# FFN products as three one-pass products of 12-bit parts, in place of seven full-precision products for eight

## The chip, the cores and the metric

The kernel runs on one core of one Trainium2 chip. The core has five engines that work side by side: TensorE (PE, matrix products; its weight loads are listed as PEld), VectorE (DVE), ScalarE (ACT), GpSimd (POOL), and SyncE (SP), which here starts most of the transfers. Matrix products go to PSUM[...]. The metric is the time of one execution on the device, in microseconds (us); lower is better. Before the change it is 296.61 us, the median of three runs (296.38 to 301.45). The profiled execution, from which the rows below come, spanned 300.1 us.

## The reference, cut to what matters

Two parts run one after the other: a chunked state-space scan (batch 4, 8 heads, 768 tokens, head dimension 32, state 16), and on its output a feed-forward network (FFN) with a maximum over three products.

```python
# x (4, 8, 768, 32), a (4, 8, 768), B and C (4, 8, 768, 16); log_a = log(clip(a, 1e-6, 1))
for c in range(24):                                # chunks of 32 tokens in the reference
    cum = np.cumsum(la, axis=-1)
    L = np.exp(cum[..., :, None] - cum[..., None, :]) * causal
    y_intra = (Cc @ Bc.T * L) @ xc                 # within the chunk
    y_inter = (Cc @ state) * np.exp(cum)[..., None]    # from the chunks before
    y[:, :, sl] = y_intra + y_inter
    state = exp(sum(la)) * state + sum_j exp(cum[-1] - cum[j]) * outer(B[j], x[j])

xx = y.transpose(0, 2, 1, 3).reshape(3072, 256)
h = np.maximum(np.maximum(xx @ w1, xx @ w2), xx @ w3)   # w1, w2, w3: 256 x 768
out = h @ w_out                                         # w_out: 768 x 256
```

All of it is in 32-bit floating point. The weights arrive as 64-bit numbers, which the kernel itself decodes to 32 bits.

## The kernel before

It works in six blocks. Block c holds tokens 128c to 128c+127 of all four batches, so 512 tokens. The scan of block c+1 is woven into the FFN of block c, and the last product of the FFN (`out = h @ w_out`, here called the down product) of a block is done while the next block's FFN runs. The order of the instructions on each engine is the order of the program.

The first FFN products (the up products) of block 0 are plain: four 128 x 512 products for each weight and pair of column tiles. From the second block on they go by a scheme in which seven products of 256 columns take the place of eight, with sums of the weights and of the scan's output made beforehand, and sums of the results made afterwards:

```python
def weight_sums(k):                    # GpSimd, once for each of the 9 weight groups k
    nc.gpsimd.tensor_tensor(out=s1, in0=a21, in1=a22, op=ALU.add)
    nc.gpsimd.tensor_tensor(out=s3, in0=a11, in1=a21, op=ALU.subtract)
    nc.gpsimd.tensor_tensor(out=s2, in0=s1, in1=a11, op=ALU.subtract)
    nc.gpsimd.tensor_tensor(out=s4, in0=a12, in1=s2, op=ALU.subtract)

def products(c, k, which, first):
    for p, bank, half in which:
        nc.tensor.matmul(                                             # L628
            out=bank[:, half], lhsT=left(p, k), rhs=sides[c][p],
            start=(first and half == 0), stop=True, skip_group_check=True)

def early(c, k):
    A, B = (sum_bank(kind, [P, 2, HB]) for kind in "AB")              # HB = 256 tokens
    products(c, k, [(1, A, 0), (6, A, 1), (5, B, 0), (7, B, 1)], True)
    ...
    nc.scalar.copy(out=eu[:, 0], in_=A[:, 0])                         # L653
    nc.vector.tensor_tensor(out=eu[:, 1], in0=A[:, 1], in1=eu[:, 0], op=ALU.add)   # L654
    nc.vector.tensor_tensor(out=v, in0=B[:, 1], in1=eu[:, 1], op=ALU.add)          # L655
    nc.vector.tensor_tensor(out=t[:, 2], in0=B[:, 0], in1=v, op=ALU.add)           # L656

def late(c, k):
    products(c, k, [(2, A, 0), (3, B, 0), (4, B, 1)], False)
    if i == 0:
        nc.scalar.copy(out=m[:, 0], in_=A[:, 0])                                   # L667
    else:
        nc.vector.tensor_tensor(out=to[:, 0], in0=m[:, 0], in1=A[:, 0], op=ALU.max)  # L669
    nc.vector.tensor_tensor(                                                       # L670
        out=t[:, 0:2], in0=B, in1=eu[:, 1:2].to_broadcast([P, 2, HB]), op=ALU.add)
    if i > 0:
        return [lambda: nc.vector.tensor_tensor(                                   # L673
            out=to[:, 1:4], in0=m[:, 1:4], in1=t, op=ALU.max)]

def down_next(kind=ffn_bank):          # 3 products of 256 columns, 24 products per block
    ...
    for f in range(half * NQ, (half + 1) * NQ):
        nc.tensor.matmul(                                             # L691
            out=o[:, i], lhsT=hT[c][:, f, b * P:(b + 1) * P], rhs=wo_sb[:, f],
            start=(f == 0), stop=(f == NF - 1), skip_group_check=True)
    ...                                # then a copy to SBUF and a transfer to the output

for c in range(1, NC):                 # blocks 1 to 5
    for k in range(NW):                # 9 weight groups: 3 weights x 3 groups of 256 columns
        early(c, k)
        ...                            # a piece of the next block's scan, or down_next()
        maximum = late(c, k)
        if c == 1 and k + 2 < NW:
            weight_sums(k + 2)
        ...                            # more pieces, masks, loads
while downs:
    down_next(att_bank)                # the last block's down products, alone at the end
```

Of the scan, four kinds of work matter for the steps below. ACT takes the exponential of the decays, four instructions to a piece (L391). DVE multiplies the scores by the decays (L491). POOL masks the decays (L384). PE makes the scores (L483) and the scan's output y (L506, L519), which ACT copies out of PSUM (L543). In the decoding of the weights ACT (L175, L184), DVE (L176, L179, L188) and POOL (L185) take turns.

Of the kernel before, what the change touches and what calls it, by code (L numbers as in the profile page):

```python
# [10 lines left out]
BF16 = mybir.dt.bfloat16  # L11
U32 = mybir.dt.uint32
# [7 lines left out]
def kernel(  # L20
# [41 lines left out]

    SMALL, LARGE = 2.0 ** -15, 122880.0 - 2.0 ** -7

    const = ctx.enter_context(tc.tile_pool(name="const", bufs=1))
    raw = ctx.enter_context(tc.tile_pool(name="raw", bufs=2))
    att = ctx.enter_context(tc.tile_pool(name="att", bufs=2))
    ffn = ctx.enter_context(tc.tile_pool(name="ffn", bufs=2))
    wraw = ctx.enter_context(tc.tile_pool(name="wraw", bufs=10))
    wtmp = ctx.enter_context(tc.tile_pool(name="wtmp", bufs=3))  # L70
# [51 lines left out]
    def load(c, name):  # L122
        src, w = sources[name]
        t = blocks[c][name] = raw.tile([P, BH, w], FP32, tag="raw_" + name, name="raw_" + name)
        nc.sync.dma_start(  # L125
            out=t, in_=src[:, :, c * P:(c + 1) * P, :].rearrange("b h s n -> s (b h) n"))
# [3 lines left out]
    w_sb = [const.tile([P, KD, DF], FP32, name="w%d" % i) for i in range(3)]  # L130
    wo_sb = const.tile([P, NF, DM], FP32, name="wo")
# [4 lines left out]

    weight_jobs = []
    for f0 in range(0, DF, WCOL):
        for w, t in zip((moe_w1, moe_w2, moe_w3), w_sb):
            per = 1 if w.dtype == FP32 else 2  # L140
            src = words(w)[:, per * f0:per * (f0 + WCOL)]
            weight_jobs.append(
                (t[:, :, f0:f0 + WCOL], src.rearrange("(k p) f -> p k f", p=P), w.dtype))
    for o in range(0, NF, 2):
        weight_jobs.append(
            (wo_sb[:, o:o + 2],
             words(moe_w_out)[o * P:(o + 2) * P, :].rearrange("(o p) m -> p o m", p=P),
             moe_w_out.dtype))

    fetched = []  # L150

    def fetch():

        dst, src, dt = weight_jobs.pop(0)
        if dt == FP32:
            nc.sync.dma_start(out=dst, in_=src)
        else:
            rb = wraw.tile([P, 2, WCOL, 2], U32, tag="rb", name="rb")
            nc.sync.dma_start(out=rb.rearrange("p k f w -> p k (f w)"), in_=src)  # L159
            fetched.append((dst, rb))  # L160

    def decode_steps():


        dst, rb = fetched.pop(0)
        shape = [P, 2 * WCOL]
# [3 lines left out]
        def first():  # L170
# [3 lines left out]
            held["u"] = u = wtmp.tile(shape, U32, tag="w_u", name="w_u")  # L174
# [8 lines left out]
            r = wtmp.tile(shape, U32, tag="w_r", name="w_r")  # L183
# [19 lines left out]
    def sign():  # L203

        unsigned.pop(0)()

# [169 lines left out]
    def last_load(c):  # L376
        E = blocks[c]["E"] = raw.tile([HN, NB, P], FP32, tag="E", name="E")
# [21 lines left out]

    def scan_b(c, kind):  # L400
# [4 lines left out]
        st["BT"] = BT = att.tile([HN, NB, P], FP32, tag="BT", name="BT")  # L405
# [13 lines left out]
    def scan_c(c):  # L419
# [3 lines left out]
        st["CT"] = CT = att.tile([HN, NB, 2, P], FP32, tag="CT", name="CT")  # L423
        for g in range(2):
            nc.scalar.mul(CT[:, :, g], tr, parity[:, g:g + 1])
# [5 lines left out]
    def scan_cd(c):  # L431
# [3 lines left out]
        st["Cd"] = Cd = att.tile([HN, NB, P], FP32, tag="Cd", name="Cd")  # L435
        nc.vector.tensor_tensor(out=Cd, in0=st["trC"], in1=E, op=ALU.mult)

    def scan_bd(c):
        st = blocks[c]
        st["Bd"] = Bd = att.tile([P, BH, N], FP32, tag="Bd", name="Bd")  # L440
        nc.gpsimd.tensor_tensor(
            out=Bd, in0=st["B"], in1=from_j[c].unsqueeze(2).to_broadcast([P, BH, N]),
# [31 lines left out]
    def scan_scores(c, b0, banks=None):  # L474
# [4 lines left out]
        for i in range(2):  # L479
            b = b0 + i  # L480
            for r, s in banks.items():
# [3 lines left out]
                    rhs=st["CT"][rows, b].rearrange("p g i -> p (g i)"),  # L485
# [38 lines left out]
    def first_own(bs):  # L524
# [9 lines left out]
        if 0 not in yT:  # L534
            yT[0] = ffn.tile([P, KD, BLK], FP32, tag="yT", name="yT")
# [4 lines left out]
    def scan_y(c):  # L540
        yT[c] = ffn.tile([P, KD, BLK], FP32, tag="yT", name="yT")
        for t in range(KD):
            nc.scalar.copy(out=yT[c][:, t], in_=blocks[c]["y"][t].rearrange("p b i -> p (b i)"))  # L543

    def scan_sums(c):

        y11, y12, y21, y22 = (
            yT[c][:, k, r * HB:(r + 1) * HB] for k in range(2) for r in range(2))
        late = [blocks[c]["y"][k].rearrange("p b i -> p (b i)")[:, r * HB:(r + 1) * HB]
                for k in range(2) for r in range(2)]  # L550
        t = ysum[c % 2]
        later.extend(
            lambda k=k, a1=a1, a0=a0: nc.vector.tensor_tensor(  # L553
                out=t[:, k], in0=a1, in1=a0, op=ALU.subtract)
            for k, (a1, a0) in enumerate((
                (late[1], y11), (late[3], t[:, 0]), (late[3], y12), (late[2], t[:, 1]))))
        sides[c] = {1: y11, 2: y21, 3: y22, 4: t[:, 3], 5: t[:, 0], 6: t[:, 1], 7: t[:, 2]}


    hT = {}  # L560
    def h_of(c):
        if c not in hT:
            hT[c] = ffn.tile([P, NF, BLK], FP32, tag="h", name="h")
        return hT[c]

    def group(bank, i, f, halves):

        for r in halves:
            for k in range(KD):
                nc.tensor.matmul(  # L570
                    out=bank[:, r * HB:(r + 1) * HB],
                    lhsT=w_sb[i][:, k, f * P:(f + 1) * P],
# [3 lines left out]
    def whole_group(bank, i, f):  # L576
        for k in range(KD):
            nc.tensor.matmul(  # L578
                out=bank, lhsT=w_sb[i][:, k, f * P:(f + 1) * P], rhs=yT[0][:, k],
# [9 lines left out]
    NW = 3 * NQ  # L589
    ysum, wsum = [], {}  # L590

    def kilos(b):

        t = wraw.tile([P, 2, WCOL, 2], U32, tag="rb", name="rb").bitcast(FP32)
        return t.rearrange("p k f w -> p (k f w)").rearrange("p (a b) -> p a b", b=b)

    quarters = {}

    def places():
        for _ in range((NW + 1) // 2):  # L600
            t = kilos(P)
            for half in (t[:, 0:4], t[:, 4:8]):
                if len(wsum) < NW:
                    wsum[len(wsum)] = half
        ysum.extend(kilos(HB) for _ in range(2))

    def weight_sums(k):
        q, i = divmod(k, 3)
        a11, a12, a21, a22 = (
            w_sb[i][:, kk, (2 * q + g) * P:(2 * q + g + 1) * P]  # L610
            for g in range(2) for kk in range(2))
        s1, s2, s3, s4 = (wsum[k][:, j] for j in range(4))
        nc.gpsimd.tensor_tensor(out=s1, in0=a21, in1=a22, op=ALU.add)  # L613
        nc.gpsimd.tensor_tensor(out=s3, in0=a11, in1=a21, op=ALU.subtract)
        nc.gpsimd.tensor_tensor(out=s2, in0=s1, in1=a11, op=ALU.subtract)
        nc.gpsimd.tensor_tensor(out=s4, in0=a12, in1=s2, op=ALU.subtract)

    def left(p, k):
        if p in (1, 2, 4):
            q, i = divmod(k, 3)  # L620
            g, row = {1: (0, 0), 2: (0, 1), 4: (1, 1)}[p]
            f = 2 * q + g
            return w_sb[i][:, row, f * P:(f + 1) * P]
        return wsum[k][:, {5: 0, 6: 1, 7: 2, 3: 3}[p]]

    def products(c, k, which, first):
        for p, bank, half in which:
            nc.tensor.matmul(  # L628
                out=bank[:, half], lhsT=left(p, k), rhs=sides[c][p],
                start=(first and half == 0), stop=True, skip_group_check=True)  # L630

    later = []
# [6 lines left out]
    held = {}  # L639

    def early(c, k):
        q, i = divmod(k, 3)
        A, B = (sum_bank(kind, [P, 2, HB]) for kind in "AB")
        products(c, k, [(1, A, 0), (6, A, 1), (5, B, 0), (7, B, 1)], True)
        if i == 0:
            held["m"] = ffn.tile([P, 4, HB], FP32, tag="m", name="m")
# [331 lines left out]
```

## Time and profile before

| engine | busy us | share of the span | instructions |
|---|---|---|---|
| PE | 287.4 | 96% | 2024 |
| PEld | 225.1 | 75% | 2024 |
| DVE | 199.9 | 67% | 382 |
| ACT | 121.1 | 40% | 315 |
| POOL | 72.1 | 24% | 96 |

Busy time is that of the named engine in the span of 300.1 us. A 32-bit product stands in the trace as two pairs of weight load and product, so 315 products of the up side from block 1 on make 630 rows, and 144 down products make 288. Rows of the groups give the line of the kernel, the engine and operation, what is written and read, the shape, the number of instructions, then busy time and the mean length of one; after the bar stands the idle time just before them and what ended it. [...] DMA moved 28.13 MB in the span, at a mean of 94 GB/s.

### The profile page before, as it was taken

Reading aid. Unit: us, or ns where it says so; the run is one execution under the profiler, and the core shown is the slowest. Engines: PE = TensorE matmul, PEld = TensorE weight load, DVE = VectorE, ACT = ScalarE, POOL = GpSimd, SP = SyncE. Lnnn points to the kernel's source line nnn. Section 1 sums busy time; section 2 is a strip of 40 time slices with the busy share of each in tenths; the row PEclk is TensorE's granted clock in tenths of the full one; section 3 lists DMA queues with packets and bytes.
Section 4 is the critical chain, followed back from the end, with each engine's and each line's share of the span. In section 5 each row is a group of like instructions: output and inputs, shape, how many; then the busy total and the mean of one; then the engine's idle time right before and its main releaser. Section 6 shows DMA issues by size and latency. Waiting matters only on the chain.

```text
span 300.1 us, 5303 instructions
## 1 busy us (share of the span) xinstructions
PE 287.4 (96%) x2024; PEld 225.1 (75%) x2024; DVE 199.9 (67%) x382; ACT 121.1 (40%) x315; POOL 72.1 (24%) x96
## 2 busy tenths in 40 slices
PE   6679999999999999999999999999999999999995
PEld 4557435477677788888888888888887888888784
DVE  2752867989588556867676867676867676667540
ACT  2934687943672545334344334344330211011200
POOL 5241647468991600007000006000000000000000
PEclk9957999999999999999999999999999999999999
DMA  7989879969969105792007790001010001010101
GB/s 88 189 274 290 214 140 175 223 173 183 177 141 127 35 2 167 186 131 46 2 0 207 162 136 22 3 2 35 0 37 0 2 0 35 2 36 0 35 20 52
DMA packets 105049, 28.13 MB, mean 94 GB/s; under 512 B 75328, under 2 KB 101952, under 8 KB 105024
## 3 DMA queue, kind: packets, MB, share of 16 engines
q1 hardware_dynamic: 104144, 27.14, 45.6%
q10 hardware_dynamic: 880, 0.66, 0.7%
q8 instruction: 16, 0.26, 0.4%
q14 instruction: 9, 0.07, 0.1%
HBM read 24.54 MB, written 3.24 MB: 93 GB/s over the span
## 4 chain that ended last, share of the span: by engine, by line
PE 81%; DVE 7%; POOL 3%; DMA 3%; SPq 2%; issue 2%; ACT 1%; POOLq 0%; DVEq 0%; ACTq 0%
PE sumB L628 25%; PE o L691 19%; PE sumA L628 18%; PE up L578 5%; PE s L483 4%; DMA raw_x<-in_x_dram 3%; PE y L519 3%; DVE L L491 2%; PE up L570 2%; PE y L506 1%; POOL w_u L185 1%; PE y L530 1%; SPq L125 1%; PE A L451 1%; SPq L159 1%
## 5 line engine op out<-in xcount | busy, mean ns | idle before, releaser
L691 PE MATMUL o<-wo,h 128*128 128x256 f32 x288 | 68.9, 379 | 0.0
L691 PEld LDWEIGHTS o<-wo,h 128*128 128x128 f32 x288 | 54.7, 190 | 7.4
L628 PE MATMUL sumA<-yT,w 128*128 128x256 f32 x180 | 55.5, 390 | 0.4 <-DVE eu L654 0.3
L391 ACT ACTIVATE L<-L,ncums 128x128 f32<-128x128 f32 x160 | 50.3, 391 | 8.9 <-POOL L L384 8.9
L653 ACT COPY eu<-sumA 128x256 f32<-128x256 f32 x45 | 16.7, 372 | 89.2 <-PE sumA L628 80.6
L628 PE MATMUL sumB<-rb 128*128 128x256 f32 x180 | 46.2, 379 | 0.0
L654 DVE TENSOR_TENSOR eu<-sumA,eu 128x256 f32<-128x256 f32 x45 | 19.0, 422 | 31.1 <-ACT eu L653 31.1
L628 PEld LDWEIGHTS sumA<-yT,w 128*128 128x128 f32 x180 | 31.9, 189 | 9.4 <-issue 2.5
L628 PEld LDWEIGHTS sumB<-rb 128*128 128x128 f32 x180 | 34.2, 190 | 4.6
L491 DVE TENSOR_TENSOR L<-s,L 128x512 f32<-128x512 f32 x46 | 29.3, 680 | 3.1 <-PE s L483 2.7
L578 PE MATMUL up<-yT,w 128*128 128x512 f32 x64 | 29.1, 600 | 0.2 <-DVE w L188 0.2
L628 PE MATMUL sumB<-yT,rb 128*128 128x256 f32 x90 | 27.6, 389 | 1.6 <-DVE rb L656 1.3
L670 DVE TENSOR_TENSOR rb<-sumB,eu 128x512 f32<-128x512 f32 x30 | 20.7, 689 | 10.9 <-PE sumB L628 10.8
L628 PE MATMUL sumA<-rb 128*128 128x256 f32 x90 | 26.9, 380 | 0.3 <-DVE rb L553 0.3
L628 PE MATMUL sumB<-rb,w 128*128 128x256 f32 x90 | 26.8, 379 | 0.0
L185 POOL TENSOR_TENSOR w_u<-w_u,w_r 128x512 uint32<-128x512 uint32 x12 | 15.3, 1272 | 32.6 <-DVE w_u L179 19.0
L578 PEld LDWEIGHTS up<-yT,w 128*128 128x128 f32 x64 | 11.6, 190 | 14.7 <-issue 11.6
L655 DVE TENSOR_TENSOR v<-sumB,eu 128x256 f32<-128x256 f32 x45 | 19.1, 425 | 4.7
L384 POOL TENSOR_SCALAR_AFFINE_SELECT L<-L 128x1024 f32<-128x1024 f32 x20 | 22.2, 1138 | 0.0
L628 PEld LDWEIGHTS sumB<-yT,rb 128*128 128x128 f32 x90 | 16.1, 189 | 7.0 <-DVE rb L656 2.1
L628 PEld LDWEIGHTS sumA<-rb 128*128 128x128 f32 x90 | 17.0, 190 | 2.9 <-POOL rb L613 0.7
L628 PEld LDWEIGHTS sumB<-rb,w 128*128 128x128 f32 x90 | 17.1, 190 | 2.3
(101 smaller groups left out, 324.0 us busy)
## 6 DMA issues: line engine op xcount, KB each, us to landing
L<-cums SPq DMA_DIRECT2D x10, 1024.0 KB, 8.8
rb<-in_moe_w_dram SPq DMA_DIRECT2D x9, 512.0 KB, 7.4
raw_x<-in_x_dram SPq DMA_DIRECT2D x6, 512.0 KB, 7.8
out_dram<-ob SPq DMA_DIRECT2D x10, 256.0 KB, 2.3
raw_B<-in_B_dram SPq DMA_DIRECT2D x6, 256.0 KB, 4.9
raw_C<-in_C_dram SPq DMA_DIRECT2D x6, 256.0 KB, 6.3
rb<-in_moe_w_out_dram SPq DMA_DIRECT2D x3, 512.0 KB, 6.3
E<-cums SPq DMA_DIRECT2D x40, 32.0 KB, 3.8
```

What stands on the lines that cost most here:

```text
L185: nc.gpsimd.tensor_tensor(out=u, in0=u, in1=r, op=ALU.add)
L384: nc.gpsimd.affine_select(out=Ls[c][:, b], in_=Ls[c][:, b], pattern=[[0, NH], [1, P]], compare_op=ALU.is_ge, fill=MASKED, base=0, channel_ ...
L391: nc.scalar.activation(L[:, b, h], L[:, b, h], AF.Exp, bias=ncum[c][:, b * NH + h:b * NH + h + 1], scale=1.0)
L483: nc.tensor.matmul(out=s[:, i].rearrange("j g i -> j (g i)"), lhsT=st["BT"][rows, b], rhs=st["CT"][rows, b].rearrange("p g i -> p (g i)"), ...
L491: nc.vector.tensor_tensor(out=M, in0=s, in1=M, op=ALU.mult)
L578: nc.tensor.matmul(out=bank, lhsT=w_sb[i][:, k, f * P:(f + 1) * P], rhs=yT[0][:, k], start=(k == 0), stop=(k == KD - 1))
L628: nc.tensor.matmul(out=bank[:, half], lhsT=left(p, k), rhs=sides[c][p], start=(first and half == 0), stop=True, skip_group_check=True)
L653: nc.scalar.copy(out=eu[:, 0], in_=A[:, 0])
L654: nc.vector.tensor_tensor(out=eu[:, 1], in0=A[:, 1], in1=eu[:, 0], op=ALU.add)
L655: nc.vector.tensor_tensor(out=v, in0=B[:, 1], in1=eu[:, 1], op=ALU.add)
L670: nc.vector.tensor_tensor(out=t[:, 0:2], in0=B, in1=eu[:, 1:2].to_broadcast([P, 2, HB]), op=ALU.add)
L691: nc.tensor.matmul(out=o[:, i], lhsT=hT[c][:, f, b * P:(b + 1) * P], rhs=wo_sb[:, f], start=(f == 0), stop=(f == NF - 1), skip_group_check ...
```

## The change

The 32-bit operands of the up and down products of blocks 1 to 5 are cut in a high and a low part of 12 bits each, stored in the type float32r[...]. With TAU = 2^-12, HIGH a little below 1, `hi` the rounded high part, `lo` the (scaled) rest and `d` the difference of the two, three products (`d`d`, `hi`hi`, `lo`lo`) and one scaling of the first by -KAPPA give the whole product. The purpose is to have three products that pass the array once, summed in PSUM, in place of seven eighths of full 32-bit products; with that the sums before and after the seven products fall away. Block 0 keeps its full 32-bit products. The scan does the same arithmetic. The diff is cut to its core and shortened in places.

```diff
+F32R = mybir.dt.float32r
-    raw = ctx.enter_context(tc.tile_pool(name="raw", bufs=2))
+    raw = ctx.enter_context(tc.tile_pool(name="raw", bufs=1))     # B, x, E: 2 each; C: 1
-    wraw = ctx.enter_context(tc.tile_pool(name="wraw", bufs=10))
+    wsum = ctx.enter_context(tc.tile_pool(name="wsum", bufs=12))
+    wraw = ctx.enter_context(tc.tile_pool(name="wraw", bufs=12))

+    def weight_parts(k):               # 12 weight tiles, each 128 x 512
+        def last():
+            nc.gpsimd.tensor_tensor(out=d, in0=hi, in1=lo, op=ALU.subtract)
+        return [
+            lambda: nc.scalar.activation(hi, w, AF.Copy, scale=HIGH),
+            lambda: nc.gpsimd.tensor_tensor(out=lo, in0=w, in1=hi, op=ALU.subtract),
+            lambda: nc.scalar.activation(lo, lo, AF.Copy, scale=1.0 / TAU),
+            last]

     def scan_y(c):
-        for t in range(KD):
-            nc.scalar.copy(out=yT[c][:, t], in_=...)
-    def scan_sums(c): ...              # four DVE sums of 128 x 256, L553
+        for t in range(KD):
+            nc.scalar.activation(hi[:, t], y, AF.Copy, scale=HIGH)
+            later: nc.vector.tensor_tensor(out=lo[:, t], in0=y, in1=hi[:, t], op=ALU.subtract)
+            later: difference(d[:, t], hi[:, t], lo[:, t])

+    def difference(out, hi, lo):
+        nc.vector.scalar_tensor_tensor(
+            out=out, in0=lo, scalar=-1.0 / TAU, in1=hi, op0=ALU.mult, op1=ALU.add)

+    def hidden(f, src, soon):          # the six tiles of h, each 128 x 512
+        nc.scalar.activation(hi, src, AF.Copy, scale=HIGH)
+        (nc.vector if soon else nc.gpsimd).tensor_tensor(
+            out=lo, in0=src, in1=hi, op=ALU.subtract)
+        def rest():
+            difference(d, hi, lo)

-    weight_sums, products, early, late: gone
+    def down_scaled(bank):
+        nc.scalar.activation(bank, bank, AF.Copy, scale=-KAPPA)

+    ring = ("sumA", 1), ("sumB", 2), ("ffn", 1), ("sumB", 2)      # four PSUM banks in turn
+    AHEAD = 2
+    def unit_open(u):                  # two products of 512 columns, then the scaling
+        for kk in range(KD):
+            nc.tensor.matmul(out=o, lhsT=weight_part(k, 2, kk, cols), rhs=yT[c][2][:, kk], ...)
+        down_scaled(o)
+    def unit():                        # opens unit u + 2, then finishes unit u
+        for kk in range(KD):
+            for j in range(2):
+                nc.tensor.matmul(out=o, lhsT=weight_part(k, j, kk, cols), rhs=yT[c][j][:, kk], ...)
+        if i == 0: nc.vector.tensor_copy(out=m[g], in_=o)
+        else:      nc.vector.tensor_tensor(out=m[g], in0=m[g], in1=o, op=ALU.max)
+        if i == 2: one unit later hidden(...), and rest() one unit after that

     def down_next():
+        # "Y": the d products of two token tiles (12 of 256 columns), then down_scaled
+        # "X": the hi and lo products of the same tiles (24 of 256 columns), then the output
```

Two units, 18 to a block, stand where `early` and `late` of one weight group stood. A unit of the next block is opened only when the parts of that block's y are noted as ready, which the program does at the end of a block. The tables that say which piece of the scan or of the down products comes after which unit were set anew: block 0's down products come in the groups k = 2 and 7 of block 1, later ones in the groups 1 and 2. The parts of weights 0 to 5 are made during the FFN of block 0, those of 6 to 11 during block 1. The scan's operands, y's parts and the decoding share fixed places in memory.

## The prediction

> **What bounds the kernel now.** I read the busy shares first, then the chain that ended last, then busy time by stage, then single groups.
>
> ```profile
> PE 287.4 (96%) x2024; PEld 225.1 (75%) x2024; DVE 199.9 (67%) x382; ACT 121.1 (40%) x315; POOL 72.1 (24%) x96
> ...
> PE 81%; DVE 7%; POOL 3%; DMA 3%; SPq 2%; issue 2%; ACT 1%; POOLq 0%; DVEq 0%; ACTq 0%
> ```
>
> PE is busy nearly throughout and holds 81% of the chain. By stage (start:end, its length, then the busy time and count of PE, PEld, DVE, ACT, POOL, PE clock, DMA share, GB/s), the stages being about: start, FFN of block 0, of blocks 1 to 5, last down products:
>
> ```profile
> 0.00:26.10 26.10, 19.12 (x221) 13.29 (x221) 12.89 (x30) 12.09 (x22) 10.18 (x18) 0.81 0.94 197
> 26.10:67.30 41.20, 40.71 (x264) 21.71 (x261) 31.25 (x54) 28.95 (x68) 21.55 (x23) 1.00 0.95 195
> 67.30:113.30 46.00, 44.68 (x332) 35.23 (x331) 33.51 (x65) 23.03 (x71) 28.24 (x43) 1.00 0.63 110
> 113.30:158.00 44.70, 44.70 (x341) 37.72 (x342) 31.72 (x62) 19.05 (x53) 6.59 (x7) 1.00 0.47 89
> 158.00:203.00 45.00, 45.00 (x344) 37.90 (x342) 32.09 (x63) 18.47 (x52) 5.53 (x6) 1.00 0.46 89
> 203.00:247.50 44.50, 44.26 (x311) 37.25 (x310) 31.49 (x62) 12.49 (x32) 0.00 (x0) 1.00 0.04 13
> 247.50:286.50 39.00, 38.60 (x178) 33.18 (x177) 25.27 (x49) 5.54 (x14) 0.00 (x0) 1.00 0.06 21
> 286.50:300.10 13.60, 10.37 (x49) 8.78 (x47) 1.67 (x3) 1.49 (x4) 0.00 (x0) 0.98 0.12 40
> ```
>
> From block 1 on PE has no idle time worth the name, at full clock; the other engines are at 12 to 73%. So work taken from PE is time gained, until another engine's share of a stage nears 100%. The unit of PE work is seen in the chain in order of time (start, length):
>
> ```profile
> 286.51 10.37 PE o L691 x48
> ```
>
> 48 halves of 256-column 32-bit products in 10.37 us: 0.216 us each, 0.432 us for a whole product.
>
> [...] No run here shows a float32r product; that it takes one pass is the change's own premise. [...] The trace's loads:
>
> ```profile
> L691 PEld LDWEIGHTS o<-wo,h 128*128 128x128 f32 x288 | 54.7, 190 | 7.4
> L519 PEld LDWEIGHTS y<-L,raw_x 128*32 128x32 f32 x320 | 8.4, 110 | 0.9 <-issue 0.9
> L410 PEld LDWEIGHTS trB<-ident,raw_B 128*128 128x128 f32 x24 | 2.8, 141 | 1.0 <-issue 0.5
> ```
>
> 96 columns more (32 to 128) cost 80 ns, 0.83 ns a column[...]. The third row says that 32-bit loads can be quicker, and four transposes of 128 columns follow each other at 0.107 us with such loads hidden. [...] L188 runs 0.69 us undisturbed and 1.08 beside a mask of POOL.
>
> **The change part by part.** PE, up products. Before: 45 groups (5 blocks x 9) x 7 products x 0.432 = 136.1 us. After: 90 units x 6 one-pass products of 512 columns x 0.216 = 116.6. Gain 19.5 us, 3.9 a block. [...]
>
> PE, down products of blocks 1 to 5. Before: 120 x 0.432 = 51.8. After: 360 one-pass products of 256 columns. If the load hides, 0.11 us each: 39.6, gain 12.2 us, 2.4 a block. [...] I take it as hidden because of the transposes.
>
> So PE alone would bring 31.7 us, to 268.4 in the trace. What is given back:
>
> ACT. Removed: 45 copies L653 and 15 L667 (22.2 us). Added: 90 scalings in PSUM, 30 high parts of h, 24 weight scalings. What each costs, from the timeline (start, length):
>
> ```profile
> 28.77 0.67 ACT L175 ACTIVATE w_u<-rb 128x512 f32<-128x512 f32 x1
> 29.34 0.69 ACT L184 ACTIVATE w_r<-rb 128x512 f32<-128x512 uint32 x1
> ...
> 63.87 1.07 ACT L543 COPY yT<-y 128x512 f32<-128x512 f32 x2 [3.33 <-PE y L519]
> ...
> 75.42 1.28 ACT L391 ACTIVATE L<-L,ncums 128x128 f32<-128x128 f32 x4 [4.58 <-POOL L L384]
> ```
>
> Two 512-column operations from SBUF start 0.57 us apart (28.77, 29.34), two from PSUM take 1.07, so 0.54 each, and four exponentials 1.28. I take ACT's instructions from the order of the changed program, not from the tables alone[...]: a scaling that PE needs stands behind the exponentials listed before it. In block 1 stand: 13 pieces of exponentials 16.6, 18 scalings 9.7, 13 weight scalings 7.4, 6 of h 3.4, y 1.1, two weights' decoding 2.3, CT 1.3, E, BT and outputs 2.2: 44 us. PE in that block has 23.3 (up) + 10.4 (block 0's full down products) + 6.4 (scan: scores 2 x 1.08, y 1.03 + 1.88, transposes 0.86, state 0.4) = 40.1. So in block 1 ACT, not PE, is the longer, and it also waits for POOL between two halves of the splits of weights 9 to 11. I give block 1 a gain of 1.5 instead of 3.9. In blocks 2 and 3 ACT has 10.2 + 9.7 + 3.4 + 1.1 + 1.3 + 3.8 = 29.5 of 38: no bound, but it must be in time: unit u + 2's scaling has 2.6 us from its opening to its use.
>
> DVE. Removed a block: L653's followers L654, L655, L656 (9 x 1.27), L670 (9 x 0.69), L669 and L673 (6 x 1.38), four sums of y (1.7): 27.6 us. Added: 18 evacuations of 128 x 512 at 0.68, 6 differences of h at 0.7 to 1.1, y's parts 2.9: 20.5. Lighter in sum, but badly timed. A unit takes PE 1.29 us. Four banks in turn mean that a unit's bank is wanted again 1.29 us after the unit's last product; the results' way out takes about 0.16 (a product's mean 379 ns less its 216) and the evacuation 0.68, so the slack is 0.45. In group 3 DVE has two evacuations, two differences and two L491: 4.2 to 4.8 us against 2.6 on PE, so PE waits about 1.5. At the block's border y's last difference comes after the last unit but one (PE waits about 0.7) and three units are opened before the first can go on. The scores need banks that down outputs have just left: 1 us. In all I take 3 us a block in blocks 2 to 4, against 6.3 gained: 3.3 net, 10 for three. Block 5 has no scan: 6.3 - 0.5 = 5.8.
>
> POOL. Removed: 36 sums (18.4 us). Added: 24 weight steps at 1.27 and 28 low parts of h: 66. About 120 us of the span, no bound; but 11 of its weight steps (14 us) fall in block 0's stage, where it has 21.6 of 41.2 and DVE's decoding waits for it in order. I charge 1 us.
>
> The end. Before: 48 halves, 10.4, then copy and transfer. After: h's last tile must go through max, high part (ACT), low part and difference (DVE) before its d product, 0.9 + 0.6 + 0.7 + 0.8 = 3 us, of which 0.5 lie beside other products; then 72 products, 7.9. Sum 10.4: no gain.
>
> Sum: -1.5 - 10 - 5.8 + 1 = -16.3 in the trace. The timed median lay 3.5 below the profiled span, so 296.6 - 16.3, about 280.
>
> **The rivals.** (1) PE-bound throughout: PE is the engine at 96% and all else is slack. Then 268 in the trace, 265 timed. Against it: 44 us of ACT in block 1 and DVE's group 3. (2) The weight load becomes the bound of the down products: 190 ns instead of 110 would add 360 x 0.08 = 29 us, about 309; at 141 ns, 11 us, 291. For it: each product has its own load, and 190 is what the 32-bit loads record; against it: [...] the transposes. (3) float32r reads 4 bytes a column at half rate: 540 x 0.216 and more on top, over 390. Against it: the 141 ns loads of 32-bit data. (4) Block 0 and 1 stretch: in-order waits ACT-POOL-DVE in the splitting, 5 to 8 us more, 287.
>
> **Range and chances.** Between (1) and (4) lies most of it: 267 to 298. Faster by 2% is below 290.7. I give (2) at its full size 8%, at a part 10%, (3) 5%. Faster 0.73, same 0.13, slower 0.14.
>
> **What would show it.** The float32r products of 512 columns start 0.216 us apart and those of 256 columns 0.11; PEld's mean for them is no more than 150 ns. PE's busy share falls below 93%, with waits on ACT's scaling (block 1) and on DVE (group 3). Blocks 2 to 4 take about 41.5 us each, block 1 about 44.5, block 5 about 33, the end 13.6, block 0 about 42. Wrong if the down products are spaced over 0.15 us, if block 1 grows beyond 50, or if blocks 2 to 4 come below 39.

## The result and the profile after

The changed kernel takes 341.22 us (median of 4 runs, 341.04 to 342.51) against 296.67 before (median of 4): a ratio of 1.152, 95% interval 1.150 to 1.155. It is 44.6 us slower, where 16.6 us faster was predicted. The profile of the kernel before, like those of e3, e4, e7, e9, e11 and e12 below, has a stretch of 10.2 us at half clock between 15 and 28 us that the other profiles lack and that costs some 5 us (its span is 300.1 us, that of another execution 295.0), so the two profiles differ by less, 39.3 us, and totals below can differ by as much without the edit.

The page of the changed kernel, busy time by engine, the granted clock in 40 slices, and the chain that ended last by engine:

```profile
PE 294.3 (87%) x2054; PEld 222.0 (65%) x2054; DVE 177.2 (52%) x264; ACT 183.3 (54%) x409; POOL 126.2 (37%) x112
...
PEclk9999987999959789979969999989999799999979
...
PE 53%; DVE 16%; issue 13%; POOL 11%; ACT 5%; POOLq 0%; ACTq 0%
```

PE is no longer busy throughout (87%, before 96%). It holds 53% of the chain in place of 81%; DVE, POOL and ACT together hold 32%, although none of them is busy for more than 54% of the span. That is the mark of waits in a row over several engines, not of one engine that is full. And the clock dips again and again after the start (the digits below 9).

The busy shares by stage (start:end, length, then PE, PEld, DVE, ACT, POOL, granted clock, DMA share, GB/s). Here and below a block begins with the first up product of its FFN; the lines are blocks 0 to 4 and the end:

```profile
18.77:69.97 51.20, 43.88 (x287) 22.76 (x287) 37.14 (x57) 35.00 (x79) 33.41 (x27) 0.93 1.02 216
69.97:132.68 62.71, 51.73 (x321) 39.07 (x321) 28.22 (x41) 37.87 (x92) 32.44 (x27) 0.89 0.32 60
132.68:188.31 55.63, 49.30 (x350) 38.55 (x348) 26.54 (x39) 29.38 (x71) 20.57 (x18) 0.91 0.46 98
188.31:236.78 48.47, 45.15 (x349) 36.40 (x348) 26.56 (x39) 28.13 (x66) 15.63 (x13) 0.96 0.35 57
236.78:284.07 47.29, 44.37 (x317) 35.82 (x316) 25.76 (x38) 22.23 (x46) 7.73 (x6) 0.96 0.04 12
...
319.56:339.40 19.84, 11.30 (x73) 10.29 (x71) 3.37 (x5) 3.96 (x8) 0.00 (x0) 0.91 0.08 26
```

In block 1 ACT is busy for 37.87 of 62.71 us, DVE and POOL for less, and PE's own busy time is swollen by the clock (0.89). To separate work, clock and waits I worked out for each stage: the work of PE, which is its products times the median distance of their starts at full clock; what the stretches of half clock add to that; and the rest, the waits. All in us, rounded:

| stage | before | after | change | of it work | half clock | waits |
|---|---|---|---|---|---|---|
| start | 22.2 | 18.8 | -3.4 | 0 | -1.9 | -1.6 |
| block 0 | 42.7 | 51.2 | +8.5 | +0.1 | +1.2 | +7.2 |
| block 1 | 48.3 | 62.7 | +14.4 | -2.4 | +6.0 | +10.9 |
| block 2 | 45.1 | 55.6 | +10.5 | -4.2 | +5.0 | +9.8 |
| block 3 | 45.0 | 48.5 | +3.5 | -4.2 | +1.8 | +5.9 |
| block 4 | 44.7 | 47.3 | +2.6 | -4.2 | +1.8 | +5.0 |
| block 5 | 38.5 | 35.5 | -3.0 | -4.2 | 0 | +1.2 |
| end | 13.8 | 19.8 | +6.0 | -1.8 | +1.9 | +5.9 |
| sum | 300.1 | 339.4 | +39.3 | -21 | +15.8 | +44.3 |

The columns show what exceeds the profile before: the changed kernel's eight half-clock stretches, in which PE was busy for 38.6 us, by themselves cost about 19 us (an estimate, half of that busy time). So the one-pass products do pay, 21 us, and waits eat them twice over and slow the clock on top. The groups that matter (busy, mean ns of one, then the idle time just before and who ended it):

```profile
L718 PE MATMUL up<-six,wp 128*128 128x512 f32 x360 | 102.1, 412 | 0.4 <-ACT up L687 0.3
...
L718 PEld LDWEIGHTS up<-six,wp 128*128 128x128 f32 x360 | 71.5, 200 | 18.5 <-ACT up L687 2.7
...
L630 DVE SCALAR_TENSOR_TENSOR h<-h,h 128x512 fp32r<-128x512 f32 x30 | 33.6, 1121 | 7.7 <-POOL h L637 7.6
L637 POOL TENSOR_TENSOR h<-m,h 128x512 fp32r<-128x512 f32 x28 | 35.9, 1286 | 150.0 <-ACT h L636 149.6
```

L701 is the first product of a unit (d), L718 its other two (high and low), L766 a down product, L636, L637 and L630 the three steps that cut h: high on ACT, low on POOL, difference on DVE. The mean of an L718 product, 412 ns, is not what one costs PE: the next one starts before it ends in the record. The rows give no distance between starts; counted from the starts at full clock its median is 231 ns after an L701 (233 between the two of a unit), 227 after an L718, 120 after an L766. Scaling in PSUM (L687), which I had feared, ended 0.3 us of the waits before L718. The waits that matter in the view of waits (us in total, times, longest):

```profile
ACT wp L258 <- POOL wp L256: 14.8, 8, 4.7
...
PE s L559 <- DVE L L567: 7.2, 7, 1.9
...
PE o L766 <- DVE h L630: 6.4, 3, 2.4
...
PE y L582 <- DVE L L567: 5.1, 1, 5.1
```

The longest wait of block 1 in the timeline (start, length; the wait in brackets):

```profile
109.13 0.97 ACT L460 ACTIVATE L<-L,ncums 128x128 f32<-128x128 f32 x3
...
110.01 0.57 ACT L687 ACTIVATE up<-up 128x512 f32<-128x512 f32 x1
110.52 0.61 ACT L636 ACTIVATE h<-m 128x512 fp32r<-128x512 f32 x1
...
111.20 2.49 POOL L637 TENSOR_TENSOR h<-m,h 128x512 fp32r<-128x512 f32 x2 [2.94 <-ACT h L636]
...
112.50 1.73 DVE L630 SCALAR_TENSOR_TENSOR h<-h,h 128x512 fp32r<-128x512 f32 x1 [2.44 <-POOL h L637]
...
114.16 1.27 DVE L567 TENSOR_TENSOR L<-s,L 128x512 f32<-128x512 f32 x2
...
114.98 0.49 PE L582 MATMUL y<-six,S 32*64 32x128 f32 x4 [5.10 <-DVE L L567]
```

PE waits for L567, which has all it needs but stands on DVE behind the difference of h (L630). That waits for POOL's low part, which waits for ACT's high part, which stands on ACT behind four exponentials (the first row shows the three that reach into the stretch shown) and a scaling. The product on PE has nothing to do with h. DVE itself is idle for 2.44 us while PE waits for it. Block 0 has the same pattern with other parts:

```profile
42.32 2.78 POOL L453 TENSOR_SCALAR_AFFINE_SELECT L<-L 128x1024 f32<-128x1024 f32 x2
...
45.07 1.43 POOL L256 TENSOR_TENSOR wp<-w,wp 128x512 fp32r<-128x512 f32 x1
...
46.53 0.63 ACT L258 ACTIVATE wp<-wp 128x512 fp32r<-128x512 f32 x1 [4.69 <-POOL wp L256]
...
48.70 1.25 ACT L501 ACTIVATE six<-trC,parity 128x512 f32<-128x512 f32 x2
...
50.01 0.81 PE L559 MATMUL s<-six,six 32*128 32x256 f32 x4 [4.71 <-ACT six L501]
```

ACT stands still for 4.69 us before the scaling of a weight's low part (L258), because POOL first works through two masks; behind L258, in order, stand four exponentials and then the steps that the scores need (L501).

### The profile page after: what moved, and what is told of

It reads as the page before. It is cut to its first block, busy times and chain, and to the rows that moved or that the text cites. A ratio compares the mean times of both kernels' runs of the same rounds, so it can differ in the third digit from the quotient of the medians.

```text
span 339.4 us, 5409 instructions
## 1 busy us (share of the span) xinstructions
PE 294.3 (87%) x2054; PEld 222.0 (65%) x2054; DVE 177.2 (52%) x264; ACT 183.3 (54%) x409; POOL 126.2 (37%) x112
## 3 DMA queue, kind: packets, MB, share of 16 engines
q1 hardware_dynamic: 104144, 27.14, 39.6%
## 4 chain that ended last, share of the span: by engine, by line
PE 53%; DVE 16%; issue 13%; POOL 11%; ACT 5%; POOLq 0%; ACTq 0%
PE up L718 13%; PE o L766 12%; PE up L701 9%; PE up L657 5%; PE s L559 4%; DVE h L630 4%; POOL wd L250 3%; POOL wp L256 3%; DVE m L723 3%; DVE m L725 3%; POOL L L453 2%; PE y L595 2%; DVE L L567 2%; ACT L L460 2%; DVE six L623 1%
## 5 line engine op out<-in xcount | busy, mean ns | idle before, releaser
L718 PE MATMUL up<-six,wp 128*128 128x512 f32 x360 | 102.1, 412 | 0.4 <-ACT up L687 0.3
L637 POOL TENSOR_TENSOR h<-m,h 128x512 fp32r<-128x512 f32 x28 | 35.9, 1286 | 150.0 <-ACT h L636 149.6
L718 PEld LDWEIGHTS up<-six,wp 128*128 128x128 f32 x360 | 71.5, 200 | 18.5 <-ACT up L687 2.7
L725 DVE TENSOR_TENSOR m<-m,up 128x512 f32<-128x512 f32 x60 | 41.0, 684 | 80.7 <-PE up L718 80.3
L687 ACT ACTIVATE up<-up 128x512 f32<-128x512 f32 x90 | 51.2, 582 | 54.6 <-PE up L701 54.5
L701 PE MATMUL up<-six,wd 128*128 128x512 f32 x180 | 62.0, 432 | 6.4 <-DVE six L630 5.8
L701 PEld LDWEIGHTS up<-six,wd 128*128 128x128 f32 x180 | 33.1, 201 | 19.3 <-DVE six L630 8.0
L723 DVE COPY m<-up 128x512 f32<-128x512 f32 x30 | 20.6, 688 | 34.1 <-PE up L718 33.3
L630 DVE SCALAR_TENSOR_TENSOR h<-h,h 128x512 fp32r<-128x512 f32 x30 | 33.6, 1121 | 7.7 <-POOL h L637 7.6
L766 PE MATMUL o<-wp,h 128*128 128x256 f32 x240 | 31.2, 287 | 1.0 <-ACT ob L782 1.0
L657 PE MATMUL up<-six,w 128*128 128x512 f32 x64 | 31.3, 635 | 0.7 <-ACT wp L258 0.5
L766 PEld LDWEIGHTS o<-wp,h 128*128 128x128 f32 x240 | 30.4, 195 | 1.7 <-ACT ob L782 1.4
L567 DVE TENSOR_TENSOR L<-s,L 128x512 f32<-128x512 f32 x46 | 30.4, 680 | 0.0
L766 PE MATMUL o<-wd,h 128*128 128x256 f32 x120 | 18.8, 304 | 7.4 <-DVE h L630 6.4
L766 PEld LDWEIGHTS o<-wd,h 128*128 128x128 f32 x120 | 17.3, 207 | 9.5 <-DVE h L630 7.3
L636 ACT ACTIVATE h<-m 128x512 fp32r<-128x512 f32 x30 | 18.7, 624 | 8.8 <-DVE m L725 8.8
L218 POOL TENSOR_TENSOR six<-six 128x512 uint32<-128x512 uint32 x12 | 15.3, 1271 | 20.9 <-DVE six L212 10.5
## 6 DMA issues: line engine op xcount, KB each, us to landing
raw_x<-in_x_dram SPq DMA_DIRECT2D x6, 512.0 KB, 10.9
```

The source lines that it names most:

```text
L567: nc.vector.tensor_tensor(out=M, in0=s, in1=M, op=ALU.mult)
L630: nc.vector.scalar_tensor_tensor(out=out, in0=lo.bitcast(FP32), scalar=-1.0 / TAU, in1=hi.bitcast(FP32), op0=ALU.mult, op1=ALU.add)
L637: (nc.vector if soon else nc.gpsimd).tensor_tensor(out=lo, in0=src, in1=hi.bitcast(FP32), op=ALU.subtract)
L657: nc.tensor.matmul(out=bank, lhsT=whole[3 * (f // 2) + i][:, k, f % 2 * P:(f % 2 + 1) * P], rhs=yT[0][:, k], start=(k == 0), stop=(k == KD ...
L687: nc.scalar.activation(bank, bank, AF.Copy, scale=-KAPPA)
L701: nc.tensor.matmul(out=o, lhsT=weight_part(k, 2, kk, cols), rhs=yT[c][2][:, kk], start=(kk == 0), stop=(kk == KD - 1), skip_group_check=True)
```

## The experiments

My theory after the result (A): the parts of h and of the weights, made in steps over three engines that each work in order (idle for 2.44 and 4.69 us behind a first instruction in the two timelines), hold back other work that PE needs; the half clock follows from the waits. Rivals: (B) the one-pass products are themselves no gain; (C) POOL's slow step (1286 ns on average) and DVE's longer step beside it (1121 ns), not the order, make the wait; (D) the half clock comes by itself. Except where three rounds are named, each is one execution with a profile, beside the kernel before on the same chip.

**Leave out the weights' low parts (e1_hi_only).** The high part stands in for all three; scaling, low part and difference of the weights are not done.

```diff
+        parts[k] = 3 * [parts[k][0]]
         return [
             lambda: nc.scalar.activation(hi, w, AF.Copy, scale=HIGH),
-            lambda: nc.gpsimd.tensor_tensor(out=lo, in0=w, in1=hi..., op=ALU.subtract),
-            lambda: nc.scalar.activation(lo, lo..., AF.Copy, scale=1.0 / TAU),
-            last]
+            lambda: None, lambda: None, lambda: None]
```

> The changed kernel, but of each weight only the high part is made (one ACT step); the low part, its scaling and the difference (two POOL steps, one ACT step a weight) are left out, and the high part stands in for all three. Products, their number and their order stay. Theory A (the making of the weights' parts, a chain ACT-POOL-ACT-POOL on engines that work in order, stretches blocks 0, 1 and 2): block 0 from 51 to about 45 us, block 1 from 63 to about 50, block 2 from 56 to about 49, in all 341 to about 316. Rival (block 1 is held up by ACT's exponentials and by DVE's in-order waits, which stay): at most 8 us less, about 334.

327.09 us, between the two sums expected. Blocks 0 and 1, with the columns of the stages above:

```profile
18.60:60.69 42.09, 40.68 (x286) 21.43 (x286) 32.79 (x57) 32.44 (x74) 19.73 (x17) 1.00 0.97 219
60.69:123.07 62.38, 49.16 (x320) 38.15 (x321) 26.54 (x41) 34.38 (x85) 17.42 (x15) 0.89 0.49 90
```

Block 0 is 42.1 (was 51.2), so the 4.69 us on ACT and its like are the weights' parts. Block 2 is 48.9 (was 55.6). Block 1 is unchanged at 62.4, but for another reason: with block 0 shorter its transposes wait 7.1 us for a load of C. The change had made that buffer single, and moved its load behind others; in the changed kernel itself this lay hidden behind the longer block 0.

**Keep PE busy before a wait (e2_warm).** Eight bf16 products without use go ahead of the second half of the scores in blocks 2 to 4.

```diff
+        if b0 == 2 and c > 2:
+            for _ in range(8):
+                nc.tensor.matmul(out=banks[0]..., lhsT=ident16, rhs=mask..., start=True, stop=True)
```

> The changed kernel with eight products more in each of the blocks 2 to 4 (bf16, 128 x 512, a constant by a constant, into a bank that the scores overwrite next), put just ahead of the second half of the scores, where PE waits 2 to 3 us for a bank. Theory B (a wait of 2 to 3 us lets the clock fall to half for 3.4 us or more, and that costs as much again as the wait): the half-clock stretches that follow these waits in blocks 2 to 4 are gone, 5 to 6 us less, about 335.5, although PE has 24 products more. Rival (the clock falls for another reason, by load or by time): the stretches stay and the time is the same or up to 3 us more.

338.11 us. Blocks 2, 3, 4 take 52.8, 50.0 and 45.7 (were 55.6, 48.5, 47.3), 2.9 less in sum with 5.2 more work. Two of the four half-clock stretches in these blocks are gone, and that of block 3 is longer (6.8 us, was 3.4). The expectation calls theory B what is here the second half of A, that the waits bring the half clock; the run speaks for it, but does not settle it.

**Make the last parts in another order (e3_end).** Both maxima first, then both high parts, both low parts, both differences; the d products of the first four tiles of h meanwhile.

```diff
+                for f, src in pair.items(): nc.scalar.activation(hs[f][0], src, AF.Copy, scale=HIGH)
+                for f, src in pair.items(): nc.vector.tensor_tensor(out=hs[f][1], in0=src, in1=hs[f][0]..., op=ALU.subtract)
+                for f in pair: difference(hs[f][2], hs[f][0], hs[f][1])
```

> The changed kernel with another order at its end alone: the maxima of the last two tiles of h first, then both high parts, both low parts, both differences; and the d products of the four finished tiles of h for all tokens ahead of those of the last two. Nothing is left out. If the end lost its time to the serial chain maximum, high part, low part, difference, twice, and to the half clock after it: 4 to 6 us less, about 336. If the end is bound by its 72 products and the outputs' transfer: under 1.5 us.

342.92 us in all. The end, which alone is touched, falls from 19.8 to 16.0: 1.9 of half clock and 2.0 of waits are gone, just under the 4 to 6 us expected.

**Full down products, h not cut (e4_full_down).** The down products of blocks 1 to 5 are as before the change, w_out is not cut either.

```diff
-            def start(f=2 * q + g, src=m[g]):
-                rest = hidden(f, src, last)
...
+            hs[c, f] = hidden_place(f, c % 2, FP32)
+            nc.vector.tensor_tensor(out=hs[c, f], in0=m[g], in1=o, op=ALU.max)
```

> The up products as in the changed kernel, the down products of blocks 1 to 5 as full 32-bit products as before: h is not split (30 ACT, 28 POOL, 32 DVE steps fewer), nor is w_out (3 of the 12 weights). Nothing is left out. PE has about 1.8 us more work a block than the changed kernel. If h's parts on DVE and POOL[...] make the waits of groups 0, 3 and 6 and the end: blocks 2 to 4 lose 4 to 6 us each, the end 4, block 1 up to 10, in all about 315. If the scan and the evacuations alone make the waits: 341 to 350, for PE has 9 us more to do.

314.18 us. Block 1 takes 50.0, blocks 2 to 4 45.7, 46.0 and 44.7, the end 15.3, and from block 1 to the end of block 5 the clock never falls:

```profile
74.97:125.01 50.04, 45.64 (x321) 34.84 (x321) 23.91 (x37) 32.21 (x82) 23.41 (x21) 1.00 0.36 66
125.01:170.72 45.71, 44.47 (x326) 35.08 (x324) 20.37 (x33) 25.08 (x63) 7.43 (x8) 1.00 0.58 122
```

These are blocks 1 and 2, with the columns of the stages above. PE has more work than in the changed kernel, and every block from 1 to 4 is shorter. But blocks 2 to 4 are no shorter than before the change (45.1, 45.0, 44.7), although PE has some 2.6 us less work in each: PE still waits about 0.7 us a block for DVE in the scores and 0.4 for y's parts, and no run takes the rest apart.

**One-pass down products, h not cut (e5_no_h_parts).** Only the high part of h is made and stands in for all three.

```diff
-        (nc.vector if soon else nc.gpsimd).tensor_tensor(out=lo, in0=src, in1=hi..., op=ALU.subtract)
-        def rest():
-            difference(d, hi, lo)
-        return rest
+        hs[f] = [hi, hi, hi]
+        return lambda: None
```

> The changed kernel with h's low part (POOL) and difference (DVE) left out: ACT makes the high part and it stands in for all three operands of the down products, which stay one-pass. Theory A (the chain ACT high, POOL low, DVE difference, and DVE kept in order behind it, makes the waits of blocks 1 to 4 and of the end, and those waits bring the half clock): block 1 falls from 62.7 to about 50 us, blocks 3 and 4 from about 48 to 44, the end from 19.8 to about 15.5, block 0 stays at about 51; total about 310. Theory B (the one-pass down products themselves are slow to feed, whatever makes the parts): blocks 3 and 4 stay above 47, total above 325.

305.99 us. Blocks 1 to 3 and the end:

```profile
68.96:123.89 54.93, 50.41 (x321) 38.30 (x321) 24.00 (x37) 37.55 (x92) 27.21 (x24) 0.91 0.42 73
123.89:168.38 44.49, 42.99 (x349) 34.74 (x348) 20.37 (x33) 29.10 (x71) 11.09 (x11) 1.00 0.62 124
168.38:212.62 44.24, 42.68 (x350) 34.78 (x348) 20.37 (x33) 28.03 (x66) 6.60 (x7) 1.00 0.35 61
...
289.63:304.27 14.64, 9.81 (x73) 8.80 (x71) 0.69 (x1) 3.96 (x8) 0.00 (x0) 0.98 0.11 36
```

From block 1 to the end it takes 235.3 us against 269.4 in the changed kernel: 34.1 us for 28 steps of POOL and 32 of DVE, whose busy time is 36 and 35 us and which lie on engines that are about half idle. That is theory A for blocks 2 to 5 and the end, against B. Block 1 keeps 54.9, 5 above what I expected, where e4 has 50.0. Its waits are not longer than e4's (6.3 and 6.0 us in the view of waits), but it has 10.2 us at half clock, in which PE is busy throughout, so 5.1 us are lost, and e4's block 1 has none.

**Both left out (e6_no_parts).** e1 and e5 together: the ceiling of the one-pass products.

> Both kinds of parts left out: h's low part and difference, and the weights' scaling, low part and difference; high parts stand in, all products of the changed kernel stay. It is the ceiling of the change on TensorE. Theory A (elementwise parts cause all the loss, the one-pass products gain about 21 us of TensorE work): block 0 about 42, block 1 46 to 50, blocks 2 to 4 about 43, block 5 about 35, end about 15.5; total about 288, under the kernel before. Theory B (the one-pass products are no gain, float32r weight loads hold them up): over 297.

300.71 us, nearly 13 above what I expected. The span is 40.4 us shorter than the changed kernel's (299.0 against 339.4), but 4.0 longer than that of the kernel before in the same series (295.0). Blocks 0 and 2 to 5 came about as expected (42.1; 44.5, 44.2, 42.9; 34.0). Block 1 took 57.7, and the view of waits says why:

```profile
PE trC L484 <- DMA raw_C<-in_C_dram: 6.8, 1, 6.8
PE up L694 <- DVE six L628: 3.9, 6, 1.2
```

It is the load of C again, with 3.4 us lost to half clock around it. Without those 10.2 the span would be about 288.8 (299.0 - 10.2, an estimate), 6.2 under the kernel before. So even with the cutting free, which it can't be, the change would bring some 2%.

**The low parts on DVE (e7_h_low_dve).** Nothing is left out.

```diff
-        (nc.vector if soon else nc.gpsimd).tensor_tensor(
+        nc.vector.tensor_tensor(
```

> All low parts of h are made by DVE instead of POOL, nothing is left out. If the wait is one of POOL's long step and of DVE and POOL holding each other up (DVE difference 1.1 us on average, 0.7 undisturbed): block 1 falls by 5 us or more and the total to about 325 to 332. If it is DVE's load in order (its queue gets some 28 more operations of about 0.7 us): total the same within 5 us or longer, block 1 over 60.

346.0 us; from block 1 to the end 269.3 against 269.4, no change, and block 1 is at 65.6. The difference of h is quicker without POOL beside it (790 ns on average in place of 1121). But DVE now waits 2.70 us for ACT's high part itself and PE waits 3.50 and 3.78 us in place of 5.10 once. So C alone does not explain the loss: with the step off POOL, DVE waits in order for ACT and the time is the same. But DVE got 28 steps more (30 low parts of 0.8 us on average), so DVE's longer step beside POOL may still have a share in the changed kernel's loss.

**Does a wait bring the half clock? (e11_wait).** e4, whose blocks run at full clock, with 4, 6 and 8 extra DVE steps in front of y's products in blocks 2, 3, 4.

```diff
+        if (b0, r) == (2, NP - 1):
+            for _ in range({3: 4, 4: 6, 5: 8}.get(c, 0)):
+                nc.vector.tensor_tensor(out=M, in0=M, in1=M, op=ALU.max)
```

> The version with full 32-bit down products (314.2, no half clock in blocks 1 to 5), with 4, 6 and 8 extra DVE steps of 0.6 us in blocks 2, 3 and 4, on which the products of y wait: PE waits of about 1.0, 2.3 and 3.5 us more. If a wait of 2 us or more brings half clock after it: block 2 grows by its wait alone (45.7 to about 46.7), block 3 (46.0) by 2.3 plus 1.7 to about 50, block 4 (44.7) by 3.5 plus 1.7 to 3.4, to 50 or 51.5, with half-clock stretches of 3.4 or 6.8 us in blocks 3 and 4 only. If the clock does not hang on the waits: the blocks grow by the waits alone, 46.7, 48.3 and 48.2.

The waits came out at 1.67, 3.12 and 4.72 us, longer than aimed at. Their sum and the longest, then the three blocks and the two half-clock stretches by stage:

```profile
PE y L598 <- DVE L L570: 9.5, 3, 4.7
...
125.56:173.33 47.77, 44.87 (x326) 35.22 (x324) 23.16 (x37) 25.09 (x63) 7.45 (x8) 1.00 0.56 112
173.33:224.40 51.07, 46.39 (x326) 36.35 (x324) 24.51 (x39) 23.92 (x58) 6.60 (x7) 0.97 0.32 56
224.40:276.25 51.85, 45.78 (x293) 36.06 (x292) 25.55 (x40) 18.19 (x38) 0.00 (x0) 0.93 0.03 11
...
217.20:220.60 3.40, 3.40 (x10) 2.63 (x9) 1.19 (x2) 1.47 (x4) 0.00 (x0) 0.50 0.00 0
265.00:271.80 6.80, 4.39 (x27) 3.35 (x28) 2.26 (x4) 1.67 (x3) 0.00 (x0) 0.50 0.00 0
```

Block 2 kept full clock and grew by 2.1 us. Block 3 grew by 5.1 us, 2.0 more than its wait, and PE's 3.40 busy us at 0.50 make 1.7 of that; block 4 by 7.2, 2.4 more than its wait, with 4.39 busy us at half clock (2.2), in a stretch that began inside the wait. D falls for these blocks: the half clock is the waits' own second bill.

**Why 227 and 120 ns (e10_bf16).** e6 with bf16 operands in the one-pass products (their digits are not kept).

> The version without parts (300.7), its one-pass products with bf16 operands in place of float32r (numbers not kept). If the 11 to 17 ns by which float32r products stand further apart than I predicted (227 and 233 in place of 216 for 512 columns, 120 in place of 110 for 256) come from the 195 ns weight load of 4-byte words: spacing falls to 216 and 110 or less, load under 150 ns. If it is a fixed cost of each one-pass product: spacing stays at 227 and 120.

The distances are 216 and 109 ns, the load's mean 99 ns in place of 191 (the row of the loads for the high and low up products):

```profile
L711 PEld LDWEIGHTS <-wp 128*128 128x128 bf16 x360 | 35.7, 99 | 44.5 <-issue 3.3
```

So the 11 to 17 ns are no fixed cost of a one-pass product; they come with 4-byte operands. That it is the load and not the streamed side is likely, not shown, as both changed. The whole took 290.56 us, with C's load waited for 9.1 us.

**Repairs (e8_late_split, e9_best, e12_best).** All three keep one-pass up products only, with full down products, and give each token tile of the last down products its own PSUM bank.

```diff
# e8: three weights cut in block 0, six in block 1 (were six and three of these nine)
-        if n > 6:
-            split((n - 7) // 2 if n % 2 else None)
+        if n > 12:
+            split((n - 13) // 2 if n % 2 else None)
# e9: C's buffer double again and its load early; the scores' second half a unit later; y's parts two to a unit
# e12: from n > 10 (four weights in block 0); the scores back; pop(2) also before them
-            pop(1)
+            pop(2 if k == 3 or k > 5 else 1)
```

> Candidate: down products of blocks 1 to 5 full 32-bit as before the change in the second run series (no parts of h), three of the nine weight tiles split in block 0 and six in block 1 instead of six and three, and a PSUM bank of its own for each token tile at the end. Against the version with full 32-bit down products alone (314.2): if the weight parts stretch block 0, it falls from 54 to about 46 and block 1 grows from 50 by under 3; total 303 to 308. If block 0's length comes from something else in it, block 0 stays above 50 and the total at 312 or more.

308.02 us. Block 0 fell from 54.2 to 43.2, about 6 of it half clock, but block 1 rose to 58.2: PE waited 5.9 us for the load of C.

> Candidate: the late-split version (308.0) with raw_C double-buffered and its load issued early as in the kernel before (it waited 6.1 us for that load in block 1, and lost 3.7 us to half clock after it), the second half of the scores one step later (they waited 1.8 us a block for DVE), and y's parts emitted two to a step near the end of a block (up products waited 0.7 us and more for them). If those waits are what is left of the change's loss: block 1 at about 49, blocks 2 to 4 at 43 each, total 287 to 294, faster than the kernel before. If the waits only move to the next place: 298 to 303, no gain over the kernel before.

308.42 us in three rounds (308.09 to 314.3), ratio to before 1.042, interval 1.040 to 1.044. The waits moved: the scores, one unit later, made the state's products wait 1.6 us in blocks 2 and 3, and in block 1 an up product waited 3.1 us for POOL's difference of a weight. Blocks 4 and 5 gained a little (44.0, 34.9 against 44.7, 35.8 in e8). In e9 and e12 the first two units of a block are opened before the block before has ended; their blocks 2 to 5 are counted from 2 to 3 us after the first up product, with the same number of products as elsewhere.

> The last candidate (308.4) with the weights' parts started one step earlier (four of nine tiles in block 0; an up product had waited 3.2 us for POOL's difference in block 1, and half clock followed), the scores back in their place, and a second small DVE step emitted in the unit before them, so that their banks are free. If the waits named were the loss: block 1 falls from 57.3 to about 50, blocks 2 and 3 from 47.8 to about 44, total 292 to 298, level with the kernel before or a little faster. If POOL's load in blocks 0 and 1 moves the wait again: block 1 over 54, total over 300.

300.28 us in three rounds (299.1 to 304.28), ratio 1.012, interval 1.007 to 1.016. Block 1 is at 50.0, the blocks after it at 45.6, 45.6, 44.3 and 34.9. From the first up product of block 1 to the end its profile takes 234.2 us, that of the kernel before 235.2; the start and block 0 take 68.4 against 64.9. So the first blocks still pay: the weights' parts are in block 0, and at the head of block 1 PE waits 2.6 and 1.1 us for y's parts. The best version here is about level with the kernel before (1.2% longer) and does not beat it.

## Why the prediction was wrong

The step that failed is the charge for what the new parts cost: I added up the busy time of ACT, DVE and POOL, took them to be lighter or half idle, and charged a few us of waits. The runs showed chains in order over these engines on which PE waits (44.3 us more in all than before, by the table above), and half clock after the waits; with both kinds of parts left out (e6) 40.4 us are gone. The terms one by one:

**PE's gain, 31.7 us predicted, 21 measured.** Right in kind: a float32r product of 512 columns stands in the trace as one row, its starts 227 ns apart, where a full one in block 0 takes two rows 429 ns apart. The steps "x 0.216" and "0.11 us each" were mis-sized; that one pass takes a quarter of the 0.432 us of a full product of 256 columns was my estimate, with no float32r product in the trace before to show it. Up: 180 x 0.231 + 360 x 0.227 = 123.3 in place of 116.6. Down: 360 x 0.120 = 43.2 in place of 39.6. These 10.3 us are the difference. Rival (2) was the right worry at a small size: the load's mean is 195 to 207 ns, and products still start 120 apart. The recorded length of a load is not the time that it costs; my mark "no more than 150 ns" was a bad test. Rival (3) fell.

**"Block 1 a gain of 1.5", the step that failed most: it lost 14.4.** I summed ACT's busy time to 44 us and called ACT the longer engine. ACT was busy for 37.9 of 62.7 us, 6 less than I had summed. The longest wait, 5.10 us, is the chain over ACT, POOL and DVE in the timeline above (0.9 in e4 and in e5), and half clock adds 6.0. e4 took 12.7 us of the block away, e5 7.8; some 3 us of waits for y's parts stay in both.

**"3 us a block in blocks 2 to 4": 9.8, 5.9 and 5.0 of waits, and 5.0, 1.8 and 1.8 of half clock.** I compared how much DVE had to do in a group with how long PE took, which gives 1.5 us. I did not ask what DVE waits for at the head of its queue, nor what stands behind it there. I had the order on ACT in the text ("a scaling that PE needs stands behind the exponentials listed before it") and used it only to add up. The two timelines show what it costs: DVE idle for 2.44 us and ACT for 4.69 us behind a first instruction that waits for POOL.

**"I charge 1 us" for the weights in block 0: 8.5, of which 7.2 are waits.** The sum of POOL's time was right (33.4 of 51.2 us busy), but ACT waited 4.69 us for one of its steps. Leaving the steps out gave 9.1 back. Rival (4), 5 to 8 us for blocks 0 and 1 together, named the mechanism and had a third of the size, since the two lost 22.9.

**The end, no gain predicted, 6.0 lost.** My 3 us for the last tile's parts is what one tile takes. I left out that the tile before it goes through the same steps in order (PE waited 1.6 and 2.4 us), and the half clock after it. e3 gave 3.8 back.

**The half clock, in no term of the sum: 15.8 us.** In the profile of the changed kernel the half-clock stretches last 3.4 or 6.8 us, in that of the kernel before the one stretch lasts 10.2 (each profile has one more that begins in its last 0.6 us), and all 17 changes of the clock in the first and all 3 in the second lie on a grid of 3.413 us. The half clock came after waits, but not by their length alone: in the changed kernel a wait of 1.87 us in the scores of block 2, with 0.53 us more soon after, was followed by 6.8 us at half clock; in e11 1.67 us was not. Cut along this grid, the two profiles together have 168 pieces of 3.413 us at full clock: half clock came after all 9 in which PE was busy for less than 50%, after 2 of the 8 with 50 to 74%, and after none of the 151 above. So where a wait falls on the grid counts too; what decides between 50 and 74% stays open.

**Block 5, "about 33": 35.5,** the smallest miss of the blocks. PE's smaller gain, 4.2 us in place of 6.3, makes most of it; nothing of the scan is left there to wait.

## What to carry to other kernels

When work moves from a full engine to three that are half idle, add up neither their busy time nor their share. Follow each new chain through the queues in order, and ask at each hop what stands behind the waiting instruction and whether the full engine needs it. Expect to pay for a wait of TensorE twice: where it left PE busy for less than half of a 3.413 us piece of the clock's grid, half clock followed in 9 of 9 cases in the profiles before and after, and 3.4 us of it cost up to 1.7 us (e11: 3.40 busy us at 0.50). And when a stage gets shorter, look for the load that it had hidden, as with C here.

## What the runs showed of the hardware

A float32r product stands as one row in the trace of the changed kernel, its starts 227 (512 columns) and 120 ns (256 columns) apart, where bf16 gives 216 and 109 (e10). The weight loads of those 256-column products last 195 to 207 ns on average in the record, and the products still start 120 ns apart. A DVE difference of two operands in SBUF takes 0.68 us with POOL idle (12 of the 30 of h) and mostly 1.4 to 1.7 beside a POOL operation (14 of them; the average of all 30 is 1121 ns). Avoiding it by moving the step gained nothing (269.3 against 269.4). In the profiles before and after the clock changed only on a grid of 3.413 us (20 changes), and it went to half only after pieces of the grid in which PE was busy for less than 75% (11 of 17 such pieces, none of the 151 above).
